# Attention with sorted blocks and a Fourier mixer: keys of two heads in one tile, block means inside the first transform

## The chip, the cores and the metric

One Trainium2 chip, one of its cores. The metric is the device time of one execution in microseconds (us). The engines are named as in the profile: PE is TensorE's matrix multiply and PEld its weight load, DVE is VectorE, ACT is ScalarE, POOL is GpSimd, SP is SyncE, which here only issues DMAs.

## The reference, cut to what matters

```python
# q, k, v: (4, 8, 768, 64); sort_net: (4, 8, 8, 8); 8 blocks of 96 rows
P = sort_net; five rounds of: exp, divide by row sums, divide by column sums
k_sorted = einsum('bhij,bhjcd->bhicd', P, k_blocks)      # the same for v
scores = 0.125 * q_block @ k_sorted_block.T              # inside each block of 96
attn = softmax(scores);  x = attn @ v_sorted_block       # (4, 768, 512) over all heads
u = x + real(fft(fft(x, axis=1), axis=2))
un = (u - mean(u)) / sqrt(var(u) + 1e-6)
out = u + relu(un @ w_ch1) @ w_ch2                       # 512 -> 2048 -> 512
```

## The kernel before

Four batches (b) pass one after the other through the same stages. Every stage is recorded as a list of steps, each with an engine or a choice of engines, a cost, the tiles that it reads and writes, and a priority worked out from its batch and the length of the work behind it. A list scheduler (class `Plan`) then writes the instruction order of all engines. A table of due times per step name and batch, `LEAD`, shifts the priorities. Once written, each engine's order is fixed: an engine that waits for an operand holds everything behind it.

The stages that matter here, with their step names and lines before:

- `means(b)`: sums of v over positions become block means. `psaT` (L638) makes them with 64-wide weights, DVE writes them as a high and a low float16 part into `amt` (L645, L646), and `psA` (L632) turns them into `a16`. The attention is worked out without its mean: `vo` subtracts `a`, and the mean's part of the output is added again later.
- `q_mix` (`psQ`, L707) turns q around, two heads in one tile `qT` of 128 rows (64 rows of each head). `k_mix` (`psK`, L726) sorts k the same way into PSUM, and two evictions (`kz`, L480 on ACT or L484 on DVE) write it to `kzs[hp]`, which has one half of its columns for each head; the other head's 64 rows are zero there. So a product of `qT` with a half of `kzs` over all 128 rows takes the right head alone.
- Scores, one head (all 8 blocks) at a time. Batches 0 and 1: `maxima` (`psS`, L784), then `scores`, in which eight products bring in minus the maximum (L800) and eight the scores (`psT`, L803), exp on ACT (L808), minus one into `eT`. Batches 2 and 3: `turned` (`psS`, L821), exp with the maximum as bias (L826), and a transposing DMA from `es` to `eT` on SP's queue (L845). `values` (`psN`, L868) multiplies by the sorted v in `vs`, which came over DMAs (L690), and DVE normalises into `xr` (L874, L875).
- `fold` (L892, L897) adds and subtracts the two halves of the sequence, `dft_s` (`psWo` L913, `psWe` L925 to L934) is the transform over the sequence, by tables `cso` and `cse` of 96 rows, four blocks to a product group; its results are `W`.
- `mean_path`: `psM` (L746, L751) transforms the means over the model axis by `cdh` and its low part `cdl`, `mh` (ACT) and `tm` (L759, DVE) evict them. `dft_d` (`psF`, L966 to L982) is the transform over the model axis; its first product (L966) adds the means' part by the table `lm`.
- `residual`, `add_res` on POOL (L1032, L1033), statistics, `un`, and its transposes into `unT`, by PE (L1101) or a DMA (L1091).
- `mlp`, for two groups of 384 rows in each batch: 64 products of L1129 and 48 of L1150 for a group. Its priority lies behind all attention steps of later batches, so it fills what they leave free.

Of the kernel before, what the change touches and what calls it, by code (L numbers as in the profile page):

```python
# [9 lines left out]
F32 = mybir.dt.float32  # L10
F16 = mybir.dt.float16
# [5 lines left out]
H = 8  # L17
# [3 lines left out]
BLK = 96  # L21
G = 6
# [22 lines left out]
def _consts():  # L45
# [9 lines left out]
    cd_lo = (cd - cd_hi.astype(np.float64)).astype(np.float16)  # L55
    chunk = lambda m: np.ascontiguousarray(
        m.reshape(2, 128, 2, 3 * LT).transpose(1, 0, 2, 3))
    cd_hi, cd_lo = chunk(cd_hi), chunk(cd_lo)
# [17 lines left out]
    kall = np.concatenate([kpl.reshape(-1), [384]])  # L76
    sall = np.arange(S)
    anga = 2.0 * np.pi * ((sall[:, None] * kall[None]) % S) / S
    csum = np.cos(anga).reshape(NB, BLK, 385).sum(1)
    ssum = -np.sin(anga).reshape(NB, BLK, 385).sum(1)  # L80

    lm = np.zeros((128, 2, 2, 385), np.float16)
    for e, m in enumerate((csum, ssum)):
        hi = m.astype(np.float16)
        lo = (m - hi.astype(np.float64)).astype(np.float16)
        for r, w in enumerate((hi, hi, lo, lo, hi, hi)):
            lm[8 * r:8 * r + 8, 0, e] = w
            lm[64 + 8 * r:72 + 8 * r, 1, e] = w
    negm = np.zeros((128, 1), np.float32)
    negm[32:64] = negm[96:128] = -1.0  # L90
# [17 lines left out]
    for r, kr in enumerate(KP):  # L108
# [12 lines left out]
    return (mask8, selj, mask16, cd_hi, cd_lo, cse, cso, lm, negm, vrow, ones, idx, rsel,  # L121
            nident)
# [260 lines left out]
def kernel(  # L383
# [13 lines left out]
    names = ("mask8", "selj", "mask16", "cdh", "cdl", "cse", "cso", "lm", "negm", "vrow", "ones", "idx",  # L397
             "rsel", "nident")
    (mask8_d, selj_d, mask16_d, cdh_d, cdl_d, cse_d, cso_d, lm_d, negm_d, vrow_d, ones_d,
     idx_d, rsel_d, nident_d) = [  # L400
# [44 lines left out]
    ring("xs", 2, [BLK, 4, 128], F16)  # L445
    ring("x4", 2, [BLK, 2, 2, 128], F16)
# [13 lines left out]
    ring("mh", 1, [128, 2, 2 * LT], F16)  # L460
# [103 lines left out]
    lm = const.tile([128, 2, 2, 385], F16, name="lm_sb")  # L564
    junk = lm[:, 0].rearrange("p e k -> p (e k)")[:, 0:DM]
# [16 lines left out]
    kzs = [const.tile([128, 2, S], F16, name=f"kz{i}") for i in range(4)]  # L582

    def clear_kz(i):
        nc.scalar.activation(kzs[i].rearrange("p h s -> p (h s)"),
                             junk[:, 0:1].broadcast_to([128, 2 * S]), AF.Copy, scale=0.0)
# [10 lines left out]
    cse = const.tile([BLK, 2, 386], F16, name="cse_sb")  # L597
    nse = const.tile([BLK, 2, 192], F16, name="nse")
    cso = const.tile([BLK, 4, 384], F16, name="cso_sb")
    cdh = const.tile([128, 2, 2, 3 * LT], F16, name="cdh_sb")  # L600
    cdl = const.tile([128, 2, 2, 3 * LT], F16, name="cdl_sb")
    negm = const.tile([128, 1], F32, name="negm_sb")
# [13 lines left out]
    amt = const.tile([128, 4, 128], F16, name="amt")  # L616
    a16 = const.tile([128, DM], F16, name="a16")
    amr = const.tile([128, 4, 128], F16, name="amr")
    tm = const.tile([128, 2, 2 * LT], F16, name="tm")
# [6 lines left out]
    def means(b):  # L626
# [12 lines left out]

        def gT(e):  # L640
            ps = bank(pT, [128, 4, NB])
            amv = amt[:, :, 64 * (b % 2):64 * (b % 2) + 64].rearrange(
                "p t (x y i) -> p t x y i", x=4, y=2)
            pTb = ps[:, :, None, :].broadcast_to([128, 4, 4, NB])
            nc.vector.tensor_copy(amv[:, :, :, 0, :], pTb)  # L645
            nc.vector.tensor_tensor(amv[:, :, :, 1, :], pTb, amv[:, :, :, 0, :], op=ALU.subtract)  # L646
# [6 lines left out]
            ("amt", b, {"V": 640}, gT, [pT], [("amt", b % 2)]))  # L653
        plan.chain(
            ("psA", b, {"T": 260}, fA, ["amr"], [pA]),
            ("a16", b, {"A": 585, "V": 685}, lambda e: copy(e, a16, bank(pA, [128, DM])), [pA], ["a16"]))

# [58 lines left out]
    def k_mix(b, hp):  # L716
# [12 lines left out]
        def ev(e, hh):  # L729
            r = slice(64 * hh, 64 * hh + 64)  # L730
            copy(e, kzs[hp][r, hh].rearrange("x (i g c) -> x i g c", g=G, c=16),
                 six(r).rearrange("x g (c i) -> x i g c", c=16), SCALE if b < TURN else -SCALE)
        plan.chain(("psK", b, {"T": 545}, f, [k16[b, hp], (kron[b], hp // 2)], [pK]),
                   *[("kz", b, {"A": 790, "V": 950}, lambda e, hh=hh: ev(e, hh), [pK],
                      [("kz", hp, hh)]) for hh in range(2)])

    def mean_path(b, e_):
        if e_ == 0:
            mh[b] = Buf("mh")
        pM = Buf("bank")  # L740

        def f(e):
            ps = bank(pM, [128, 2 * LT])
            for c in range(2):
                for ci, cc in enumerate((cdh, cdl)):
                    nc.tensor.matmul(ps, amt[:, c, :], cc[:, c, e_, LT:],  # L746
                                     start=(c == 0 and ci == 0), stop=False, skip_group_check=True)
            for c in range(2):
                for ci, cc in enumerate((cdh, cdl)):
                    for y in range(2):  # L750
                        nc.tensor.matmul(ps[:, LT * y:LT * y + LT], amt[:, 2 + c, :],  # L751
                                         cc[:, c, e_, LT * (1 - y):LT * (2 - y)],
                                         start=False, stop=(c == 1 and ci == 1), skip_group_check=True)
        amts = [("amt", y) for y in range(2)]
        plan.chain(
            ("psM", b, {"T": 900}, f, amts + ["cdh", "cdl", "negm"], [pM]),
            ("mh", b, {"A": 372, "V": 400}, lambda e: copy(e, mh[b].t[:, e_, :], bank(pM, [128, 2 * LT])),
             [pM], [(mh[b], e_)]),
            ("tm", b, {"V": 480}, lambda e: nc.vector.scalar_tensor_tensor(  # L759
                tm[:, e_, :], mh[b].t[:, e_, :], negm, bank(pM, [128, 2 * LT]),  # L760
                op0=ALU.mult, op1=ALU.add), [pM, (mh[b], e_)], [("tm", e_)]))
    mh = {}
# [11 lines left out]

    def maxima(n):
        b, h = divmod(n, H)
        hp, hh = h // 2, h % 2
        mxs[n] = Buf("mxs")
        pS = Buf("pair")

        def f(e):
            ps = pair(pS, BLK, 128)
            for i in range(NB):
                nc.tensor.matmul(ps[0:wide(i).stop - BLK * i, i // 4, i % 4], qT[b, hp].t[:, wide(i)], kzs[hp][:, hh, cols(i)])  # L784
        plan.chain(
            ("psS", b, {"T": 370}, f, [qT[b, hp]] + [("kz", hp, hh)], [pS]),
            ("max", b, {"V": 945}, lambda e: nc.vector.tensor_reduce(
                mxs[n].t.rearrange("p (t j) -> p t j", t=2), pair(pS, BLK), axis=AX.X, op=ALU.max),
                [pS], [mxs[n]]))

    def scores(n):
        b, h = divmod(n, H)
        hp, hh = h // 2, h % 2
# [3 lines left out]
        def f(e):  # L797
# [4 lines left out]
            for i in range(NB):  # L802
                nc.tensor.matmul(ps[0:wide(i).stop - BLK * i, i // 4, i % 4], kzs[hp][:, hh, wide(i)], qT[b, hp].t[:, cols(i)],  # L803
                                 start=False, stop=True, skip_group_check=True)
# [5 lines left out]
                [pS], [sms[n]]))  # L810

    def turned(n):
        b, h = divmod(n, H)
        hp, hh = h // 2, h % 2
        eT[n] = Buf("eT")
        et, mn, sm, pS = eT[n], Buf("mns"), Buf("sm"), Buf("pair")
# [581 lines left out]
```

## Time and profile before

| | |
|---|---|
| time, median of 3 runs | 316.94 us (312.82, 316.96, 316.94) |
| span of the profiled execution | 312.2 us (no other time of this execution is given) |
| busy PE / PEld | 287.7 us (92%) / 181.9 us (58%) |
| busy DVE / ACT / POOL | 218.6 (70%) / 206.3 (66%) / 137.8 us (44%) |
| mean granted PE clock | 0.985 |
| chain that ended last | PE 59%, DVE 15%, ACT 8%, DMA 5%, issue 5% |

A busy PE in this table includes the latency of a product's last columns, so it is no measure of streaming; the distance between the starts of products in a full queue is. The chain is followed back from the last instruction to what released it at each step. A group's line gives its number of instructions, busy time, mean ns of one, and the idle time of its engine just before.

### The profile page before, as it was taken

Reading aid. Unit: us, or ns where it says so; the run is one execution under the profiler, and the core shown is the slowest. Engines: PE = TensorE matmul, PEld = TensorE weight load, DVE = VectorE, ACT = ScalarE, POOL = GpSimd, SP = SyncE. Lnnn points to the kernel's source line nnn. Section 1 sums busy time; section 2 is a strip of 40 time slices with the busy share of each in tenths; the row PEclk is TensorE's granted clock in tenths of the full one; section 3 lists DMA queues with packets and bytes.
Section 4 is the critical chain, followed back from the end, with each engine's and each line's share of the span. In section 5 each row is a group of like instructions: output and inputs, shape, how many; then the busy total and the mean of one; then the engine's idle time right before and its main releaser. Section 6 shows DMA issues by size and latency. Waiting matters only on the chain.

```text
span 312.2 us, 7389 instructions
## 1 busy us (share of the span) xinstructions
PE 287.7 (92%) x2715; PEld 181.9 (58%) x2715; DVE 218.6 (70%) x489; ACT 206.3 (66%) x486; POOL 137.8 (44%) x206
## 2 busy tenths in 40 slices
PE   8879599999999798999998999999999999999990
PEld 5657577866765454555654767646556755645540
DVE  6779779998997888787579999997466764010010
ACT  6587587999884567998676759887715754704500
POOL 8634166957125899446444115462021763112020
PEclk9999979999999999999999999999999999999996
DMA  7975886999699776996997444569334337314021
GB/s 214 172 189 92 172 208 96 171 207 219 129 141 213 194 229 111 144 243 171 180 225 132 104 119 96 147 188 212 75 92 135 104 100 215 80 67 136 0 101 35
DMA packets 54396, 45.72 MB, mean 146 GB/s; under 512 B 23393, under 2 KB 46144, under 8 KB 54360
## 3 DMA queue, kind: packets, MB, share of 16 engines
q1 hardware_dynamic: 39560, 28.68, 36.0%
q0 software_dynamic: 14800, 16.57, 30.6%
q8 instruction: 21, 0.34, 0.5%
q14 instruction: 15, 0.12, 0.2%
HBM read 35.33 MB, written 12.58 MB: 153 GB/s over the span
## 4 chain that ended last, share of the span: by engine, by line
PE 59%; DVE 15%; ACT 8%; DMA 5%; issue 5%; POOL 4%; SPq 1%; POOLq 0%; DVEq 0%; ACTq 0%
PE bank L1129 21%; PE bank L1150 21%; DVE kz L484 3%; PE bank L913 3%; DMA v<-in_v_dram 2%; DMA eT<-es 2%; ACT kz L480 2%; PE bank L868 2%; POOL u L1032 1%; POOL u L1033 1%; PE bank L982 1%; PE bank L821 1%; DVE xr L875 1%; ACT un L1075 1%; SPq L690 1%
## 5 line engine op out<-in xcount | busy, mean ns | idle before, releaser
L1129 PE MATMUL bank<-unT,w1sb 128*128 128x384 f16 x512 | 90.8, 326 | 1.3 <-ACT hr L1135 1.3
L1150 PE MATMUL bank<-w2sb,hr 128*128 128x512 f16 x384 | 90.5, 379 | 0.6 <-DVE W L482 0.6
L1135 ACT ACTIVATE hr<-bank 128x384 f16<-128x384 f32 x128 | 60.4, 495 | 28.6 <-PE bank L1129 27.6
L1129 PEld LDWEIGHTS <-w1sb 128*128 128x128 f16 x512 | 48.3, 98 | 31.8 <-issue 2.0
L1173 POOL DMA_INDIRECT out_dram<-outt,idx_sb x23 | 23.1, 1005 | 81.9 <-DVE outt L1158 61.5
L1150 PEld LDWEIGHTS <-hr 128*128 128x128 f16 x384 | 35.9, 98 | 38.3 <-issue 0.8
L1158 DVE SCALAR_TENSOR_TENSOR outt<-ur,bank 128x512 f32<-128x512 f32 x24 | 16.4, 682 | 38.8 <-PE bank L1150 38.8
L826 ACT ACTIVATE sm<-bank,mns 96x96 f32<-96x96 f32 x128 | 32.6, 354 | 4.8 <-DVE mns L831 4.6
L1050 DVE BATCH_NORM_STATS2 st<-u 96x6 f32<-96x512 f32 (+1 forms) x32 | 21.9, 683 | 4.2 <-POOL u L1033 4.0
L875 DVE TENSOR_TENSOR xr<-bank,rz 96x512 f16<-96x512 f32 x32 | 22.0, 686 | 1.1
L1032 POOL TENSOR_TENSOR u<-u,P 96x257 f32<-96x257 f32 (+1 forms) x16 | 11.9, 743 | 22.8 <-DVE P L990 10.9
L524 POOL TENSOR_TENSOR v<-v 128x384 f32<-128x384 f32 x11 | 11.1, 1013 | 18.3 <-ACT v L478 18.2
L484 DVE TENSOR_SCALAR kz<-bank 64x768 f16<-64x768 f32 x16 | 15.2, 952 | 4.9 <-ACT kz L480 3.4
L478 ACT COPY u<-bank 96x512 f32<-96x512 f32 (+1 forms) x21 | 12.1, 586 | 9.0 <-PE bank L1009 6.5
L1075 ACT ACTIVATE un<-u,nm,rstd 96x512 f16<-96x512 f32 (+1 forms) x16 | 13.0, 819 | 6.9 <-DVE nm L1064 6.9
L913 PE MATMUL bank<-cso_sb,xs 96*128 96x384 f16 x64 | 13.4, 332 | 3.9 <-ACT sm L808 2.7
L478 ACT CAST W<-bank 128x384 f16<-128x384 f32 (+1 forms) x29 | 10.6, 402 | 8.6 <-PE bank L913 6.1
L682 DVE SCALAR_TENSOR_TENSOR vo<-a,bank 128x384 f16<-128x384 f16 x32 | 15.7, 542 | 0.0
L480 ACT ACTIVATE kz<-bank 64x768 f16<-64x768 f32 x16 | 12.7, 803 | 4.3 <-DVE kz L484 3.2
L831 DVE TENSOR_REDUCE mns<-bank 96x8 f32<-96x768 f32 x16 | 14.9, 943 | 0.7 <-PE bank L821 0.7
L892 DVE TENSOR_TENSOR xs<-xr 96x512 f16<-96x512 f16 x32 | 14.6, 469 | 0.7 <-PE bank L929 0.2
L808 ACT ACTIVATE sm<-bank 96x768 f32<-96x768 f32 x16 | 12.8, 800 | 3.5 <-PE bank L803 2.8
(149 smaller groups left out, 539.9 us busy)
## 6 DMA issues: line engine op xcount, KB each, us to landing
u_dram<-u SPq DMA_DIRECT2D x32, 192.0 KB
ur<-u_dram SPq DMA_DIRECT2D x24, 256.0 KB
v<-in_v_dram SPq DMA_DIRECT2D x11, 384.0 KB
vs<-vo SPq DMA_DIRECT2D x48, 65.0 KB
k<-in_k_dram POOLq DMA_DIRECT2D x15, 192.0 KB, 4.4
q<-in_q_dram POOLq DMA_DIRECT2D x15, 192.0 KB, 5.0
w1sb<-in_moe_w_ch_dram POOLq DMA_DIRECT2D x4, 512.0 KB, 6.9
w2sb<-in_moe_w_ch_dram POOLq DMA_DIRECT2D x4, 512.0 KB, 6.0
```

The costliest lines, as they stand in the source:

```text
L478: nc.scalar.copy(dst, src)
L480: nc.scalar.activation(dst, src, AF.Copy, scale=scale)
L484: nc.vector.tensor_scalar(dst, src, scale, None, op0=ALU.mult)
L826: nc.scalar.activation(sm.t[:, i], pair(pS, BLK)[:, y, i % 4], AF.Exp, bias=mn.t[:, i:i + 1], scale=-1.0)
L875: nc.vector.tensor_tensor(xr2[b % 2][0:BLK, :, D * h:D * (h + 1)].rearrange("p (t j) d -> p t j d", t=2), ps[:, :, :, 0:D], r[:, :, :, Non ...
L913: nc.tensor.matmul(ps, xs[b, hp, 1].t[:, j, :], cso[:, j, :], start=(j == 0), stop=(j == 3))
L1050: nc.vector.bn_stats(st.t[0:n], us[b, i, m].t[0:n])
L1129: nc.tensor.matmul(ps, w1sb[:, mc, 128 * fc:128 * fc + 128], unT[b, gr].t[:, mc, :], start=(mc == 0), stop=(mc == 3))
L1135: nc.scalar.activation(dst, bank(pH, [128, 384]), AF.Relu)
L1150: nc.tensor.matmul(ps, hr[f4].t[:, fc % 4, 128 * t:128 * (t + 1)], w2sb[:, fc, :], start=(fc == 0), stop=(fc == 15))
L1158: step("outt", b, {"V": 687}, lambda e, t=t, pC=pC, o=o: nc.vector.scalar_tensor_tensor(o.t, ur[t].t, RSC, bank(pC, [128, DM]), op0=ALU.mu ...
L1173: step("store", b, {"G": 1050}, lambda e: nc.gpsimd.indirect_dma_start(out=out.rearrange("b s m -> (b s) m"), out_offset=bass.IndirectOffs ...
```

## The change

The zero halves of `kzs` go: each tile holds 64 rows of one head and 64 of the other, is written by one eviction, and is no longer cleared. A score step no longer takes eight blocks of one head but four blocks (`y`) of both heads of a pair, and each product runs over the 64 rows of one head, the heads taking turns. `values` follows the same grouping, and so does the normalisation.

The mean path goes (`psM`, `mh`, `tm`, the product L966, the tables `lm`, `cdl`, `negm`). Instead the tiles that the first transform reads (`xso`, `xse`, now kept for a whole batch) have 24 more rows: the block means' high part twice and their low part, against 24 more rows of `cso` and `cse` that hold the block sums of the transform's factors. `psB` brings the means to those rows (16 products with 32 weights into PSUM rows 96 to 127), one copy takes them to `xso` (`xom`), one more to `xse` (`xem`). Of the four blocks of a product group the first runs over 120 rows, the others over 96.

The planner's costs for the new steps are given anew; the table `LEAD` is as before.

```diff
-    kzs = [const.tile([128, 2, S], F16, name=f"kz{i}") for i in range(4)]
-    def clear_kz(i): ...
+    kzs = [const.tile([128, S], F16, name=f"kz{i}") for i in range(4)]
...
-        def ev(e, hh):
-            r = slice(64 * hh, 64 * hh + 64)
-            copy(e, kzs[hp][r, hh]..., six(r)..., SCALE if b < TURN else -SCALE)
+        def ev(e):
+            copy(e, kzs[hp]..., six(slice(0, 128))..., SCALE if b < TURN else -SCALE)
...
-            for i in range(NB):
-                nc.tensor.matmul(ps[0:wide(i).stop - BLK * i, i // 4, i % 4],
-                                 qT[b, hp].t[:, wide(i)], kzs[hp][:, hh, cols(i)])
+    def products(ps, left, right, hp, y, start):
+        for j in range(4):
+            for hh in range(2):
+                r, w = slice(64 * hh, 64 * hh + 64), wide(4 * y + j)
+                nc.tensor.matmul(ps[0:w.stop - w.start, hh, j], left[r, w],
+                                 right[r, cols(4 * y + j)],
+                                 start=start, stop=True, skip_group_check=True)
...
+        def fB(e):
+            for t in range(4):
+                nc.tensor.matmul(pB.t[BLK:128, 128 * t:128 * t + 128], amt[:, t], ident)
...
+            ("psB", b, {"T": 260}, fB, ["amt"], [pB]),
+            ("xom", b, {"A": 585, "V": 685}, lambda e: copy(
+                e, xso[b % 2][BLK:KM, :, 0, :], ...), [pB], [("xom", b % 2)]))
+        step("xem", b, {"V": 420}, more, r=[("xom", b % 2)], w=[("xem", b % 2)])
...
-    def mean_path(b, e_): ...
...
+        rows_of = lambda j: KM if j == 0 else BLK
-                    nc.tensor.matmul(ps, xs[b, hp, 1].t[:, j, :], cso[:, j, :],
-                                     start=(j == 0), stop=(j == 3))
+                    n = rows_of(j)
+                    nc.tensor.matmul(ps, x[0:n, j], cso[0:n, j, :], start=(j == 0), stop=(j == 3))
...
-                nc.tensor.matmul(ps[0:n], lm[:, b % 2, e_, k0:k0 + n], tm[:, e_, :], start=True,
-                                 stop=False, skip_group_check=True)
...
-            ("psS", b, {"T": 370}, ...      -            ("psT", b, {"T": 730}, ...
+            ("psS", b, {"T": 190}, ...      +            ("psT", b, {"T": 550}, ...
-            ("psF", b, {"T": 680 if b else 1100}, f,
+            ("psF", b, {"T": 460 if b else 880}, f,
...
-        for h in range(H):
-            n = H * b + h
+        for hp in range(4):
+            for y in range(2):
+                n = b, hp, y
```

More of the change, by code (lines that the diff above doesn't have):

```diff
@@ L727, in f @@
                                      kron[b].t[:, 2 * hp + hh].rearrange("p c i -> p (c i)"))
[L729 to L732 removed]
+        def ev(e):
+            copy(e, kzs[hp].rearrange("x (i g c) -> x i g c", g=G, c=16),
+                 six(slice(0, 128)).rearrange("x g (c i) -> x i g c", c=16), SCALE if b < TURN else -SCALE)
         plan.chain(("psK", b, {"T": 545}, f, [k16[b, hp], (kron[b], hp // 2)], [pK]),
[L734 to L762, printed above, removed]
+                   ("kz", b, {"A": 790, "V": 950}, ev, [pK], [("kz", hp)]))
     mxs, sms, eT = {}, {}, {}
@@ L1332 @@
             mix(0)
-        if b in (0, 1):
-            for y in range(2):
-                mean_path(b, y)
         if b + 1 < B:
```

231 lines of the change are left out of this document (109 added, 122 removed).

## The prediction

> **What bounds the kernel now.** I read the page first: the span, the engines' shares, the slices and the chain that ended last; then busy time by stretches of time; then the groups by line with shapes kept apart; then the timeline of TensorE (PE) where the changed steps stand. The page:
>
> ```profile
> span 312.2 us, 7389 instructions
> PE 287.7 (92%) x2715; PEld 181.9 (58%) x2715; DVE 218.6 (70%) x489; ACT 206.3 (66%) x486; POOL 137.8 (44%) x206
> PE   8879599999999798999998999999999999999990
> PEclk9999979999999999999999999999999999999996
> PE 59%; DVE 15%; ACT 8%; DMA 5%; issue 5%; POOL 4%; SPq 1%; POOLq 0%; DVEq 0%; ACTq 0%
> ```
>
> PE is busy nearly everywhere and is 59% of the chain. The stretches show where that is a bound and where it only looks so:
>
> ```profile
> 30.00:40.00 10.00, 6.57 (x114) 5.69 (x111) 7.35 (x16) 6.24 (x10) 1.73 (x3) 1.00 0.86 179
> 40.00:50.00 10.00, 9.72 (x111) 7.21 (x109) 8.44 (x19) 8.35 (x16) 5.08 (x8) 0.83 0.77 173
> 60.00:70.00 10.00, 8.85 (x101) 6.51 (x99) 9.62 (x26) 9.14 (x21) 7.09 (x11) 1.00 1.06 200
> 100.00:110.00 10.00, 8.40 (x78) 4.83 (x77) 8.40 (x16) 5.23 (x12) 8.49 (x12) 1.00 0.81 183
> 160.00:170.00 10.00, 8.58 (x101) 4.84 (x100) 9.29 (x15) 7.14 (x19) 6.46 (x10) 1.00 0.98 176
> 180.00:200.00 20.00, 20.00 (x179) 13.39 (x178) 19.35 (x48) 16.42 (x53) 6.70 (x9) 1.00 0.50 129
> 262.00:301.00 39.00, 39.00 (x214) 20.77 (x213) 5.11 (x9) 15.68 (x32) 5.30 (x6) 1.00 0.29 93
> ```
>
> The columns are the stretch, its length, busy PE, weight loads, DVE, ACT, POOL (each with a count), the granted clock, the DMA share and GB/s. Up to about 70 us PE waits for DVE, ACT and DMAs. From then on the MLP products fill every hole that the attention leaves, from 180 us PE is full, and from 262 us only MLP is left:
>
> ```profile
> 262.62 10.40 PE bank L1129 x64
> 273.02 10.36 PE bank L1150 x48
> ```
>
> These pieces of the chain, in order of time, give a product's price in a full queue: 10.40/64 = 0.1625 us for 384 columns and 10.36/48 = 0.216 for 512 (the group means of section 5 hold the latency too). So the end is the sum of what PE must stream, plus its waits before 180 us. Work taken from PE shortens the run wherever it lies after 70 us; work taken from DVE or ACT only where PE waits.
>
> **The change, part by part.**
>
> *The mean path on PE goes.* Its rows, and the timeline where they run:
>
> ```profile
> L746 PE MATMUL bank<-cdh_sb,amt 128*128 128x258 f16 x12 | 3.0, 273 | 0.0
> L751 PE MATMUL bank<-cdh_sb,amt 128*128 128x129 f16 x24 | 3.0, 220 | 0.0
> L966 PE MATMUL bank<-tm,lm_sb 128*96 128x258 f16 x24 | 6.5, 273 | 0.3 <-DVE P L990 0.3
> 30.69 0.28 PE L746 MATMUL bank<-cdh_sb,amt 128*128 128x258 f16 x1
> 30.80 0.27 PE L746 MATMUL bank<-cdl_sb,amt 128*128 128x258 f16 x1
> 31.14 0.28 PE L751 MATMUL bank<-cdh_sb,amt 128*128 128x129 f16 x2
> 31.25 0.28 PE L751 MATMUL bank<-cdl_sb,amt 128*128 128x129 f16 x2
> ```
>
> Starts lie 0.11 us apart for 258 columns and 0.055 for 129. With the equal groups on cdl that is 24 x 0.11 + 48 x 0.055 = 5.3 us; on L966 there are 32 products (24 of 96 rows, 8 of 97), 32 x 0.11 = 3.5 us. **-8.8 us.** In exchange the first transform's products get 120 rows instead of 96 for one of its four blocks:
>
> ```profile
> L913 PE MATMUL bank<-cso_sb,xs 96*128 96x384 f16 x64 | 13.4, 332 | 3.9 <-ACT sm L808 2.7 <-DVE xs L892 1.0
> L678 PE MATMUL bank<-v,kron 128*128 128x384 f16 x32 | 6.9, 326 | 0.1
> L632 PE MATMUL bank<-ident,amr 128*128 128x128 f16 x16 | 1.6, 220 | 0.3
> 20.61 0.38 PE L632 MATMUL bank<-ident,amr 128*128 128x128 f16 x4
> ```
>
> A product of 384 columns takes 332 ns with 96 rows and 326 with 128: rows are free. The new step psB is 16 products of the shape of L632, (0.38 - 0.22)/3 = 0.053 us each: **+0.9 us**.
>
> *The scores.* Now, 384 products (L784, L803, L821, 128 each):
>
> ```profile
> 53.94 0.51 PE L800 MATMUL bank<-nident_sb,mxs 96*128 96x96 f16 x8
> 54.28 0.51 PE L803 MATMUL bank<-qT,kz 128*128 128x96 f16 x8
> 112.11 1.14 PE L1129 MATMUL bank<-unT,w1sb 128*128 128x384 f16 x6
> 113.18 0.53 PE L726 MATMUL bank<-kron,k 128*64 128x128 f16 x12
> 113.64 0.42 PE L1012 MATMUL bank<-xr,rsel_sb 99*96 99x512 f16 x1
> ```
>
> Eight take 0.34 us, 0.0425 each, 16.3 us in all. The change makes no fewer of them: each fills 64 of 128 rows, and two neighbours use different halves. Whether two halves of rows run at once, no row shows. Halves of columns do: L726's twelve products of 128 columns and 64 weights take 0.46 us from their start to the next group's, where one after the other they would need 12 x 0.053 = 0.64. I take the pairs at once, 0.047 us a pair (0.0425 and a few ns for the second's start): 192 x 0.047 = 9.0, **-7.3 us**. Bounds: -8.2 (0.0425 a pair) and 0 (not at once).
>
> The same rows show a price. Six products of L1129 from 112.11 end their streaming at 112.11 + 6 x 0.1625 = 113.09, and L726 starts at 113.18: 0.09 late. Within the group, 0.46 is 0.14 more than six pairs at 0.053. So going into half-array products and out again costs some 0.19 us, about 0.095 a turn. In the order in which the instructions of the two programs stand on PE, the shape of the array in use (whole, halves by column, halves by row, psB's quarter) turns 49 times before and 129 times after, since the score steps stand singly among whole-array products: 37 runs of them, 30 of eight. 80 x 0.095 = **+7.6 us**. Bounds: 0, if halves by row turn freely, and 80 x 0.11 = 8.8.
>
> [...]
>
> *DVE and ACT.*
>
> ```profile
> L484 DVE TENSOR_SCALAR kz<-bank 64x768 f16<-64x768 f32 x16 | 15.2, 952 | 4.9 <-ACT kz L480 3.4 <-PE bank L726 0.9 <-ACT a L478 0.5
> L480 ACT ACTIVATE kz<-bank 64x768 f16<-64x768 f32 x16 | 12.7, 803 | 4.3 <-DVE kz L484 3.2 <-DVE a L482 0.5 <-PE bank L726 0.4
> L759 DVE SCALAR_TENSOR_TENSOR tm<-mh,negm_sb,bank 128x258 f16<-128x258 f16 x6 | 2.8, 477 | 0.6 <-ACT mh L478 0.6
> L478 ACT CAST mh<-bank 128x258 f16<-128x258 f32 x6 | 2.2, 384 | 1.5 <-PE bank L751 1.5
> L478 ACT CAST a<-bank 128x512 f16<-128x512 f32 x3 | 1.7, 579 | 0.0
> L646 DVE TENSOR_TENSOR amt<-bank,amt 128x128 f16<-128x128 f32 x4 | 1.2, 291 | 0.1
> 38.78 0.81 PE bank L913 x4
> ```
>
> Thirty-two evictions of kz become sixteen of the same length and twice the partitions: (15.2 + 12.7)/2 = 14 us less over both engines. tm and mh drop 5.0; psB's four copies (priced as `a`, 0.58) and the four copies into xse (some 0.5) add 4.3. Behind 70 us all of this hides under the MLP products and counts nothing. Before 70 us PE's own share of the gain, 3.4 us of L746 and L751 for batches 0 and 1 and part of L966, needs DVE and ACT to move up as well. Half of the kz saving, 7 us over two engines, falls there, 3.5 an engine, so I let the PE terms stand and add nothing. Without that cover some 3 us of the gain would stay behind.
>
> *Moved and added waits; queues.* psB waits for DVE's two amt operations (291 ns each at most), and behind it on PE stands a q transpose, whose eviction leads to the maxima: half a microsecond once a batch, under MLP products in three of four. The first transform now waits for psB's copies too; the 18 us from L632 at 20.61 to the first L913 at 38.78 cover them. On SP the loads of lm, cdl and negm go (0.8 MB by their shapes), those of cse and cso grow by a quarter, and cdh's load falls behind the three copies of `a` into xr; its first reader, the second transform, comes behind that L913. The clearing of kz on POOL and ACT stands ahead of waits for v and for the sort net's chain, so taking it away frees nobody. All nothing.
>
> *The order.* One scheduler places every step from due times per step name, and these are kept. Before 180 us PE's waits may shrink by 3 (DVE and ACT lighter) or grow by 10 (first rival's price and a bit); I take 0, as the MLP tail after the last transposes is alike in both orders (64, 48, 64, 48 products).
>
> Sum: -8.8 + 0.9 - 7.3 + 7.6 = **-7.6 us**, so a span of 304.6. The page has no other time of the profiled execution. The fastest shown run, 312.82, is its span and 0.6; the other two lie 4.1 higher and are the median, 316.94, and no row tells why. I apply the difference to the median: **309.3 us** (-2.4%).
>
> **The rivals.**
>
> *PE meets a transposed eT too early (slower).* Place: batches 2 and 3, the values step L868, behind which all of PE queues.
>
> ```profile
> 29.80 7.38 DMA v<-in_v_dram
> 151.15 6.42 DMA eT<-es
> L868 PE MATMUL bank<-vs,eT 97*128 97x65 f16 x224 | 11.8, 199 | 0.8 <-DMA vs<-vo 0.7
> ```
>
> A flight of 6.42 us stands on the chain, yet L868 waited 0.8 in all: the kept due times put enough MLP ahead. They were set for steps of one head; a step is now half of two. If PE stands through a flight, the clock follows: after the 3.4 idle us of 30 to 40 it was 0.83 for 10 us, 1.7 us lost. One full stand is 8.1, two are 16.2: 325.5 us. From the second on it is slower than before. For it: due times not renewed. Against it: 0 wait after 180 us today and a lighter DVE.
>
> *The row halves do not run at once.* Then the 7.3 goes and the turns stay: 316.6, no change. For it: no row shows row halves. Against it: column halves do.
>
> *The clock gate in the early stage.* The change takes 1.8 us of products out of 30.69 to 32.5, where PE is idlest. If the clock then drops twice more at 1.7, that is 3.4 us: 312.7. Against it: one drop today. [...]
>
> **How the numbers follow.** Forecast 0.51, early eT 0.27, row halves 0.11, clock 0.11. Faster by over 2% (below 310.6; about what a measurement of this kernel can tell from no change): 0.42 of the forecast and 0.02 of the clock case, 0.44. Slower (above 323.3): 0.23 of the eT case. Within: 0.33. The range runs from 303 (turns half as dear and 3 us of waits gone) to 323, which leaves most of the second stand outside. The forecast's own range is 303 to 315.
>
> **What would show it.** Right: score groups of eight take about 0.17 us from first to last pair, with 0.09 lost on each side; PE full from 180 us; L746, L751 and L966 gone and nothing new above 1 us on PE; about 14 us less of kz; the first L1129 three to five us before 69. Wrong: second products of a pair starting 0.042 after the first (row halves); L868 waiting for eT (first rival); clock below 1.00 in more than one stretch after 10 us; turns without the 0.09, which would bring 302.

## The result, and the profile after

The changed kernel takes 321.65 us (median of five; 320.18 to 324.51), the kernel before 314.67 on the same chip: a ratio of 1.026 with a 95% interval of 1.021 to 1.031. It is slower, where the prediction said faster. The page of the profiled execution, the longest of the five at 324.51 us:

```profile
span 322.7 us, 7192 instructions
PE 291.4 (90%) x2627; PEld 176.0 (55%) x2627; DVE 214.3 (66%) x485; ACT 194.0 (60%) x470; POOL 133.5 (41%) x202
PE   8885889797968899979999999999999999999990
PEclk9999579978976599999999999999999999999996
PE 65%; DVE 11%; DMA 10%; POOL 6%; ACT 4%; issue 3%; POOLq 0%; SPq 0%; DVEq 0%; ACTq 0%
```

DVE, ACT and POOL all have less to do, as forecast, and DMA's share of the chain has doubled. The line that stands out is PEclk: before, the clock fell once (a 7); now it falls four times, and a slice goes down to 5. The stretches that answer to those of before (length, busy PE, weight loads, DVE, ACT, POOL, clock, DMA share, GB/s):

```profile
30.00:40.00 10.00, 6.55 (x73) 5.02 (x74) 5.22 (x13) 5.20 (x7) 0.00 (x0) 0.54 0.94 206
60.00:70.00 10.00, 7.94 (x129) 6.12 (x127) 8.83 (x23) 8.57 (x17) 8.85 (x13) 0.92 0.96 182
90.00:100.00 10.00, 7.79 (x91) 6.33 (x92) 5.63 (x16) 6.26 (x11) 0.93 (x2) 0.61 0.77 145
100.00:110.00 10.00, 7.31 (x56) 4.66 (x54) 6.51 (x18) 4.27 (x11) 2.84 (x6) 0.67 0.54 95
180.00:200.00 20.00, 20.00 (x179) 11.50 (x177) 19.47 (x42) 10.95 (x32) 5.09 (x6) 1.00 0.68 159
```

From 180 us on PE is full, as it was. All damage is done before 113 us. Two stands open it; the timeline of PE, then the waits of PE grouped by what ended them (in all, times, longest):

```profile
27.87 0.52 PE L758 MATMUL bank<-kz,qT 64*128 64x96 f16 x16
29.17 0.34 PE L758 MATMUL bank<-qT,kz 64*128 64x96 f16 x8
33.45 1.56 PE L842 MATMUL bank<-vs,eT 97*128 97x65 f16 x24 [3.94 <-DMA vs<-vo]
92.21 1.56 PE L842 MATMUL bank<-vs,eT 97*128 97x65 f16 x24 [2.58 <-DMA vs<-vo]
PE bank L842 <- DMA vs<-vo: 6.5, 2, 3.9
PE bank L627 <- POOL vg L521: 1.8, 1, 1.8
```

The same two places before:

```profile
33.34 0.94 PE L868 MATMUL bank<-vs,eT 97*128 97x65 f16 x24 [0.69 <-DMA vs<-vo]
80.97 0.94 PE L868 MATMUL bank<-vs,eT 97*128 97x65 f16 x24
```

The first values step of batch 0 begins at the same moment in both kernels, 33.4 us: the moves of v into `vs` set it. Before, PE came to it through the mean products (30.69 to 32.5) and waited 0.69. Now the score steps end sooner, the mean products are gone, and PE stands 3.94. The time saved there has become a wait. Batch 1's values step, in contrast, really is 11 us later.

To see what the difference is made of I added up the distances between the starts of all products of a trace. Each distance is split into the product's price at full clock (0.1625 us for 384 columns, 0.216 for 512 and in proportion; 0.0425 for 96; 0.028 for one of 64 weights, 0.022 for one of a pair of row halves), then, where the clock is half, what lies above that, up to the price once more (two products of L1105 start 0.320 us apart there, 0.162 at full clock), then gaps of up to 0.2 us, and waits above 0.2. In us, each row adding up with 1.47 to the start of the last product:

| kernel (profiled execution) | streaming | half clock | small gaps | waits | last product |
|---|---|---|---|---|---|
| before | 264.8 | 1.5 | 12.9 | 23.1 | 303.8 |
| changed | 249.0 | 14.8 | 19.6 | 29.3 | 314.2 |
| difference | -15.8 | +13.3 | +6.7 | +6.2 | +10.4 |

PE has 15.8 us less to stream and ends 10.4 later. Streaming is a count of products times a price, not a measurement of its own; the other three columns are what the trace leaves over: they say where time went, not what caused it. The profiled execution of the changed kernel is its longest, with the lowest clock of the five (0.934; the others 0.944 to 0.954), and the spans of the two traces lie 10.5 us apart where the medians lie 7.0; so its half clock is above the usual. Divided by time with the same rule (to about 1 us), 4 of the 26 us in these three columns arise before 45 us, 20 from 45 to 113 us (half clock +10, waits +9) and 2 behind that. Most is lost in batch 1's stage, not at batch 0's stand.

### The profile page after: what moved, and what is told of

Its sections match the earlier page's. It is cut to its first block, busy times and chain, and to the rows that moved or that the text cites. A ratio compares the mean times of both kernels' runs of the same rounds, so it can differ in the third digit from the quotient of the medians.

```text
span 322.7 us, 7192 instructions
## 1 busy us (share of the span) xinstructions
PE 291.4 (90%) x2627; PEld 176.0 (55%) x2627; DVE 214.3 (66%) x485; ACT 194.0 (60%) x470; POOL 133.5 (41%) x202
## 4 chain that ended last, share of the span: by engine, by line
PE 65%; DVE 11%; DMA 10%; POOL 6%; ACT 4%; issue 3%; POOLq 0%; SPq 0%; DVEq 0%; ACTq 0%
PE bank L1126 22%; PE bank L1105 20%; DMA vs<-vo 5%; PE bank L888 5%; PE bank L842 3%; DMA out_dram<-outt,idx_sb 3%; PE bank L758 2%; DMA u_dram<-u 2%; PE bank L910 2%; PE bank L958 2%; POOL u L1008 2%; DVE mxs L768 2%; PE bank L715 2%; POOL u L1009 1%; PE bank L780 1%
## 5 line engine op out<-in xcount | busy, mean ns | idle before, releaser
L1105 PE MATMUL bank<-unT,w1sb 128*128 128x384 f16 x512 | 90.9, 329 | 1.8 <-DVE vo L690 1.7
L1105 PEld LDWEIGHTS <-w1sb 128*128 128x128 f16 x512 | 48.9, 99 | 34.0 <-issue 3.3
L797 ACT ACTIVATE sm<-bank,mns 96x96 f32<-96x96 f32 x128 | 31.8, 348 | 1.2 <-DVE mns L803 1.0
L473 ACT CAST W<-bank 128x384 f16<-128x384 f32 (+1 forms) x39 | 13.0, 374 | 22.0 <-PE bank L888 9.0
L848 DVE RECIPROCAL rz<-bank 96x8 f32<-96x8 f32 x32 | 6.3, 198 | 22.2 <-PE bank L842 16.0
L842 PE MATMUL bank<-vs,eT 97*128 97x65 f16 (+1 forms) x256 | 14.5, 215 | 6.7 <-DMA vs<-vo 6.5
L842 PEld LDWEIGHTS <-eT 97*128 97x128 f16 (+1 forms) x256 | 13.5, 116 | 10.3 <-DMA vs<-vo 4.1
L827 ACT ACTIVATE eT<-sm 96x768 f16<-96x768 f32 x16 | 13.3, 841 | 6.8 <-PE bank L842 6.5
L888 PE MATMUL bank<-cso_sb,xso 120*128 120x384 f16 (+1 forms) x64 | 17.0, 400 | 0.2 <-issue 0.2
L473 ACT COPY u<-bank 96x512 f32<-96x512 f32 (+1 forms) x19 | 11.1, 593 | 7.4 <-PE bank L985 4.8
```

What stands on the lines that cost most here:

```text
L473: nc.scalar.copy(dst, src)
L797: nc.scalar.activation(sm.t[:, i], pair(pS, BLK)[:, t, i % 4], AF.Exp, bias=mn.t[:, i:i + 1], scale=-1.0)
L888: nc.tensor.matmul(ps, x[0:n, j], cso[0:n, j, :], start=(j == 0), stop=(j == 3))
L1105: nc.tensor.matmul(ps, w1sb[:, mc, 128 * fc:128 * fc + 128], unT[b, gr].t[:, mc, :], start=(mc == 0), stop=(mc == 3))
```

## The experiments

Five readings were tried against each other. **A**: the order. The scheduler's kept due times make a poor order for the new steps, PE stands, and the clock falls. **B**: half-filled products by themselves let the clock fall. **C**: the mean products had kept the clock up. **D**: the changed operations cost more than their streaming, in any order. **E**, which came out of the middle runs: the changed kernel has too little for PE to do early on, in any order. Ratios are to the kernel before on the same chip (312.5 to 315.0 us there), with 95% intervals.

### Full rows in the same order, a held load, filled waits, the keys alone

```diff
e1_full_rows (the order unchanged on all engines)
-    nc.tensor.matmul(ps[..., hh, j], left[r, w], right[r, cols(4 * y + j)], ...)
+    nc.tensor.matmul(ps[..., hh, j], left[:, w], right[:, cols(4 * y + j)], ...)
e2_kq_held, ahead of the load of q for batch 1, pair 1
+    for x in vs[0:2]:
+        nc.gpsimd.tensor_copy(landed, x[0:BLK, 0, 0:1])
e3_filled, in values()
+    for _ in range({(0, 0, 0): 18, (1, 0, 0): 12}.get(n, 0)):
+        nc.tensor.matmul(pN.t[:, 0, :], junk[:, 0:128], junk)
e5_keys_only: before, with kzs, products, maxima, scores, turned, values as changed
```

> The changed kernel with one thing altered: each score product multiplies all 128 rows of the two-head key tile instead of the 64 rows of its head (so both heads get the sum of their scores). Same instructions in the same order on every engine, no row halves, no pairs, no turns of the array for them. Theory A (the order: bulk loads stand ahead of the moves of the values, TensorE stands, its clock falls to half): the waits at L842 (6.5 us) and the stretches of half clock stay; a pair costs 0.085 us instead of 0.042, 192 of them, +8, the turns go, -8: 318 to 326 us. Theory B (half-filled products by themselves let the clock fall): the clock stays full, the 13 us of half-clock streaming come back: 308 to 314 us.

> The changed kernel; on POOL the loads of q and k for batch 1, head pair 1 (at 25.99 and 26.72 us) are held until batch 0's values have been moved into vs. Nothing else moves. Theory A: the 3.9 us of TensorE's wait at L842 near 29.5 us shrink below 1, the stretch of half clock from 30.8 to 44.5 us goes down to 7 us or less, and the run gains 3 to 8 us: 314 to 319. Theory B: the wait shrinks but the clock falls all the same: gain of 0 to 3. If neither the load nor the wait matters because DVE and ACT bound that stage: 320 to 323.

> The changed kernel with products whose result is overwritten put before the first values step of batch 0 (18 of 512 columns, 3.9 us) and of batch 1 (12, 2.6 us), where TensorE stood waiting for vs. They need no vs, so the waits stay as long as they are but TensorE is busy in them. Theory A with the clock as the price: the stretches of half clock from 30.8 and from 92.3 us go (7 to 9 us of streaming come back), the waits stay: 313 to 318. If the waits themselves are the price and the clock is not: 321 to 323. Theory B: the drops come all the same, 321 to 323.

> The kernel before with only the keys' half of the change: two heads in one key tile, scores by 64-row products, steps of half of two heads; the mean path of before stays. The scheduler places the steps anew with its kept due times. By my sum (-7.3 for pairs, +7.6 for turns, mean path unchanged): 315 to 318 if the order were as good as before. Theory A (the loss is in the order that comes out, whichever part causes it): waits above 2 us for vs or eT and more than 10 us of half clock, 318 to 326. Theory C (the mean products that were taken away had kept TensorE's clock up): one stretch of half clock as before, 314 to 318.

*Full rows*: 320.07 us, 1.019 (1.013 to 1.025). A's range, not B's: the waits at L842 stay (5.4 us) and the clock still falls, though less (20.5 us of half clock before the end, against 37.5). Streaming rises by 7.9, small gaps fall from 19.6 to 14.7, half clock from 14.8 to 8.5. Some of the half clock did go with the row halves, so B is not wholly out.

*Held load*: 318.90, 1.015 (1.009 to 1.021). The moves land 2.4 us sooner when the second pair of k/q loads keeps off them, so those loads did cost something, but not the whole wait:

```profile
31.08 1.56 PE L846 MATMUL bank<-vs,eT 97*128 97x65 f16 x24 [1.69 <-DMA vs<-vo]
```

The wait did not go below 1 and the half clock there went from 13.7 to 10.2 us, not 7: A's sign, its size at the edge. B's words fit as well (the wait shrinks, the clock falls all the same, a gain of 0 to 3), for the gain is 2.7 us, on another chip. This run does not part the two.

*Filled waits*: 320.72 (318.03 to 322.44), 1.023 (1.016 to 1.030), a miss for A, and 0.3 us short of the range for waits that cost by themselves. In the profiled execution batch 0 came as A had it: 18 products fill the stand, the values step begins where it did, the clock stays full to 91 us, and PE is 4.1 us ahead by the product that stood at 45.03 us:

```profile
29.48 4.06 PE L841 MATMUL bank<-junk 128*128 128x512 f16 x18
```

But that was the fastest of its four runs, with a mean clock of 0.979; the others had 0.959 to 0.964 and 320 to 322 us, so the clock was down for longer in them; where, no trace shows. Batch 1's half clock, 10.2 us, stayed in the profiled execution too.

*Keys alone*: 321.41, 1.021 (1.011 to 1.030), 17.1 us of half clock although the mean products are there. A's other sign, a wait above 2 us for `vs` or eT, is not there in these words: 1.1 and 0.6 us, and one of 4.0 at a values step that the trace puts down to a load of v. The half clock speaks against C as the whole cause and, with the time, for A.

### What an order is worth

```diff
e6_before_no_due / e7_after_no_due
-    LEAD = dict(P=(37.1, 31.1, 0, 0), ..., weights=(-5.3, 0, 0, 0))
+    LEAD = {}
e8_after_costs: in the changed kernel
-    ("psS", b, {"T": 190}, ...)   ("psT", b, {"T": 550}, ...)
+    ("psS", b, {"T": 370}, ...)   ("psT", b, {"T": 730}, ...)
e9_before_costs: the reverse in the kernel before
```

> The kernel before, with every due time of the scheduler's table set to zero; same work, another order. Theory A (what the change lost, it lost because due times fitted to the old steps were kept): this loses too, 318 to 332 us. Theory D (the changed operations themselves cost more than their streaming shows, whatever the order): no statement on this one; it is the base for the next.

> The changed kernel, also with every due time set to zero, so that neither kernel has an order fitted to it. Theory A: the change now shows what its work is worth, 3 to 10 us faster than the kernel before without due times. Theory D: it stays 5 to 10 us slower than that one.

> The changed kernel with the due times kept, but the scheduler is told 370 and 730 ns for the two score steps on TensorE, as for the old steps, instead of 190 and 550: what a step of eight products with its two turns really takes by the traces (0.36 and 0.71 us). If the order is poor because these costs are too low: waits at the values step under 2 us, 309 to 316. If it is poor because the due times do not fit: 316 to 324.

> The kernel before with the wrong costs of 190 and 550 ns told to the scheduler for its score steps: not one instruction is added or taken away, only the order is made anew. Theory A: 317 to 324 us, with more waits and more half clock than before. Theory D: 312 to 316.

The last is the plainest: the same operations as before (six moved from ACT to DVE), two numbers told wrongly to the scheduler, and 325.28 us, 1.039 (1.030 to 1.047), a little more than A's range. Its page:

```profile
span 321.8 us, 7385 instructions
PEclk9999999959699999999999999999999999999997
```

Without any due times the kernel before takes 324.51, 1.038 (1.031 to 1.045), and the changed one 322.34, 1.031 (1.024 to 1.038). So the kernel before loses 12 us with its fitted order, as A had it. By the sums above, its waits are then some 8 us longer and its half clock 3 (with the wrong costs 7 and 4): in this kernel a poor order costs waits first and clock second. Without due times the changed one is 0.7% ahead (2.2 us), short of A's 3 to 10. D, which had it 5 to 10 us behind, falls. Telling the scheduler the true length of the new score steps brings the changed kernel from 1.026 to 1.015 (1.008 to 1.022; 317.45 us): the given costs had left the turns out. By its expectation (309 to 316 or 316 to 324) the larger part is then in the due times, not in those costs.

### Orders fitted to the changed kernel

```diff
e10_refit, e11_refit_b, e12_refit_c: e8 with another table each
-    LEAD = dict(P=(37.1, 31.1, 0, 0), Q=(0, 1.3, 0, -8.4), ...)
+    LEAD = dict(P=(0, 183.2, 41.2, 3.1), Q=(-27.6, -56.7, 23.1, -39.0), ...)
e13_costs_filled: e8, and in values()
+    for _ in range({(0, 0, 0): 18}.get(n, 0)):
+        nc.tensor.matmul(pN.t[:, 0, :], junk[:, 0:128], junk)
```

> The changed kernel with the scheduler's due times fitted to it anew (its own table, chosen so that TensorE has work in each stretch of 3.4 us from 20 us on) and the score steps told at 370 and 730 ns. The same operations, another order. Theory A (the change's own work is worth some 9 us, and the old due times gave that and more back): below the kernel before, 304 to 312 us, with fewer than 15 us of half clock. Theory E (the changed kernel has too few products before 110 us to keep the clock up in any order): 313 to 320, with half clock between 30 and 45 us as in every kernel so far that has the row halves.

> As the run above, with a second table of due times, found from another start. Theory A: 304 to 314 us; the two tables differ by less than the 12 us that lie between the fitted and the unfitted order of the kernel before. Theory E: 313 to 320.

> As the two above, with a third table. Theory A: 305 to 315 us. Theory E: 313 to 320.

> The kernel with the old due times and the score steps told at 370 and 730 ns (317.45 us in its run), and 18 products of 512 columns, whose result is overwritten, before the first values step of batch 0, where TensorE stands waiting for vs in the stretch before the clock falls at 31.9 us. If half clock in the early stage costs time by itself: the stretch from 31.9 to 45.6 us goes (5.3 us of streaming), and the run gains 2 to 5 us: 312 to 315.5. If DVE, ACT and the moves set the pace there whatever the clock: 316.5 to 319.

312.49, 313.22 and 314.04 us: 0.999 (0.995 to 1.003), 0.999 (0.993 to 1.004) and 1.000 (0.995 to 1.006). That is 2.6 to 2.7% better than the kept table, and all three are level with the kernel before, none below. The times lie at the upper ends of A's ranges (the first half a us above): what the lower ends stood for, nine us less for PE, does not show. E's range overlaps, and its sign is there in all three:

```profile
span 309.6 us, 7184 instructions
PEclk9997569999998999999999999999999999999996
24.17:27.59 3.42, 2.40 (x60) 1.73 (x58) 3.42 (x5) 1.82 (x3) 2.95 (x7) 1.00 0.57 114
27.59:31.00 3.41, 2.78 (x40) 2.12 (x37) 2.44 (x3) 2.49 (x4) 1.33 (x2) 0.50 1.12 161
31.00:44.65 13.65, 12.72 (x127) 9.52 (x128) 8.89 (x22) 8.94 (x14) 2.69 (x4) 0.50 0.75 170
```

This is the first fitted order. In the stretch from 24.17 us, batch 0's score steps, DVE is busy throughout (3.42 of 3.42) and sets the pace; PE, with score products that take half the time, streams for 0.37 of it by the prices above, and the clock is half for the next 17 us.

The filled run missed: 320.79, 1.023 (1.017 to 1.029), where the run without filling had 1.015; slower if anything, as the intervals overlap. In its profiled execution the clock had already fallen at 27.7, so the 18 products took 6 us where PE had 2.64 to wait:

```profile
30.47 6.02 PE L841 MATMUL bank<-junk 128*128 128x512 f16 x18
33.09 1.56 PE L842 MATMUL bank<-vs,eT 97*128 97x65 f16 x24 [2.64 <-DMA vs<-vo]
```

The first row is of this run, the second of the run without filling. It came out above both alternatives, and as a test of the price of half clock it says nothing.

### Which half of the change

```diff
e14_refit_filled (count 1, 1) and e15_refit_filled_more (2, 2, and 6 in values): e10, batch 0
+    fill(pS, count)      # ahead of the products of psS, and of psT
e16_refit_full_rows: e10 with the edit of e1; e18_refit_b_full_rows: e11 with it
e4_means_only: before, with with_means, psB, xom, xem, fold, dft_s as changed, no mean_path
e17_means_refit: the same with its own LEAD, psS and psT at 370 and 730
```

> The changed kernel with the first refitted table (312.49 us), and in batch 0 one product of 512 columns, whose result is overwritten, before the products of each of the 16 score steps: 0.22 us each, about what a step lost when its products began to run in pairs (0.17). They run while TensorE waits for DVE's maxima. Theory E, sharpened (score steps of half the length leave TensorE busy in less than 0.45 of a stretch of 3.4 us near 25 us, and the clock then stays half for 10 to 17 us): half clock before 50 us falls from 17 to 7 us or less, and the run gains 2 to 5 us: 307 to 311. If that half clock lies under DVE and ACT anyway: 312 to 316.

> As the run above with two such products in each of the 16 score steps and six before the first values step, 8.2 us of them in all before 45 us. Theory E, sharpened: the clock stays full to 80 us; gain of 2 to 5 us less what does not fit under waits: 308 to 313. If half clock there costs nothing: 313 to 319.

> The first refitted order with score products over all 128 rows (both heads get the sum of their scores), no row halves, the same instructions in the same order. TensorE streams 8 us more and saves 5 of turns. Theory E, sharpened: the clock falls later or less than with the halves, and the time is 309 to 314, no more than with them: pairs gain nothing in this order. If the pairs are worth their streaming: 314 to 318.

> The changed kernel in the second refitted order (313.22 us) with score products over all 128 rows (both heads get the sum of their scores): the third order in which row halves and full rows stand in the same order. In the two others full rows were 0.6 to 0.7% below. If row halves gain nothing in any order: 309 to 313 us. If that was chance: 315 to 318 (8 us more streaming, 5 less of turns).

> The kernel before with only the means' half of the change: the 24 rows in the first transform instead of the mean path, keys and scores by head over 128 rows as before (the folded tiles are kept once, not twice, for want of memory). The order is made anew with the kept due times. By my sum (8.8 us of products out, 0.9 in): 305 to 308 us if the order were as good as before. Theory A: the order that comes out costs as much as it did the others, 316 to 326.

> The same with due times fitted to it. No row halves, so no turns for them and score steps of full length. If what the change lost after refitting lies in the row halves alone (they stream 8 us less, but turns and half clock take that back): the 8 us of the means show and the run comes to 303 to 309, below both kernels. If saved products before 110 us only lengthen the waits for moves, DVE and ACT, or the fit by hand is worse than the old one: 310 to 316.

*Filled score steps*: 313.66, 1.002 (0.998 to 1.006), and 313.41, 1.001 (0.997 to 1.005). The second did keep the clock up through the early stage, and gained nothing. The whole stretch, the first values step and a group of the first transform, each in the filled run and then in the first fitted order, and between them the last maxima on DVE in the filled run:

```profile
20.00:45.00 25.00, 24.69 (x344) 15.12 (x344) 19.66 (x38) 16.57 (x26) 9.93 (x14) 1.00 0.66 140
20.00:45.00 25.00, 21.52 (x282) 15.74 (x280) 19.04 (x38) 16.06 (x23) 9.96 (x14) 0.66 0.71 150
35.36 0.94 PE L857 MATMUL bank<-vs,eT 97*128 97x65 f16 x24
31.93 1.56 PE L851 MATMUL bank<-vs,eT 97*128 97x65 f16 x24 [1.35 <-DMA vs<-vo]
30.22 2.70 DVE L781 TENSOR_REDUCE mxs<-bank 96x8 f16<-96x768 f32 x3 [1.52 <-PE bank L771]
44.19 0.82 PE L903 MATMUL bank<-cso_sb,xso 120*128 120x384 f16 x4
44.91 0.82 PE L897 MATMUL bank<-cso_sb,xso 120*128 120x384 f16 x4
```

Clock 1.00 against 0.66 over 25 us, and the group of the first transform that stands at 44.91 us in the fitted order comes at 44.19, 0.7 us ahead. The times are those of the second alternative, and the gain of 2 to 5 us of the sharpened E did not come. But this does not show that half clock is free. The filling holds PE for 24.69 of the 25 us, DVE waits for PE's scores, and the first values step comes 3.4 us later than without filling. From there to that group the fitted order takes 13.0 us at half clock and the filled run 8.8 at full. In *filled waits* the same stage, begun at the same moment, gained 4.1. So half clock did cost some 4 us here, and the filling took most of that again.

*Full rows in two fitted orders*: 310.96, 0.993 (0.989 to 0.998), and 312.25, 0.990 (0.986 to 0.994).

```profile
span 308.9 us, 7184 instructions
PEclk9999999999999999999999999999999999999997
22.15:25.56 3.41, 3.02 (x54) 2.14 (x53) 3.41 (x9) 2.52 (x4) 2.78 (x3) 1.00 0.37 100
25.56:28.98 3.42, 3.01 (x58) 2.54 (x56) 3.42 (x6) 1.56 (x2) 2.95 (x6) 1.00 0.52 114
```

This is the first of them, among the same score steps: PE busy for 3.0 of 3.41 and the clock never down before the end. In three orders now, full rows are 0.7, 0.6 and 0.9% *below* the row halves; each pair's intervals overlap, but the sign is the same three times. The table shows where the time went in the profiled executions:

| order | | streaming | half clock | small gaps | waits | last product |
|---|---|---|---|---|---|---|
| kept due times | halves | 249.0 | 14.8 | 19.6 | 29.3 | 314.2 |
| | full rows | 256.9 | 8.5 | 14.7 | 29.4 | 310.9 |
| first fitted | halves | 249.0 | 7.8 | 18.2 | 24.7 | 301.1 |
| | full rows | 256.9 | 0.0 | 13.6 | 28.5 | 300.5 |
| second fitted | halves | 249.0 | 7.0 | 18.0 | 27.0 | 302.4 |
| | full rows | 256.9 | 4.2 | 13.6 | 26.7 | 302.8 |

The halves save 7.9 us of streaming, pay 4.4 to 4.9 for turns, and 2.8 to 7.8 in half clock.

*The means alone*: 328.10, 1.037 (1.029 to 1.045) in the order of the kept due times, even above A's range; 312.91, 0.996 (0.993 to 1.000) in one fitted to it. PE has 7.9 us less to stream (256.9 against 264.8), and 0.4% of the time shows. So the first alternative, 303 to 309, fails: the row halves are not the only place where the gain went. Both of these kernels keep the folded tiles once and not twice, which can cost waits of its own; that was not tried apart, nor is it known how good the fit is. In the trace of the fitted one, waits are 3.1 us above those of before, half clock 2.3, small gaps 1.2.

No kernel with the reference's whole computation was below the one before by more than its interval.

## Why the prediction was wrong

**The step that failed** is the one on the order, which bounded PE's waits before 180 us at 3 us less and 10 more and took 0. In the traces waits grew by 6.2, inside the bound, but of the clock the bound held no more than the 1.7 us of one stand: half clock added 13.3. Together 19.5, twice the bound, against a forecast gain of 7.6. The argument for 0, that the MLP tail is alike in both orders, looked at the end, where indeed nothing changed, and not at the stage whose order was remade. Nor did it hold that work taken from PE after 70 us shortens the run wherever it lies: by the sums above, PE streamed some 15 us less from 70 to 113 us than before, and lost as much there in half clock (10) and waits (5). The runs put the fit of an order at 12 us for the kernel before (325.28 and 324.51 against 312.53 with its own order), and at 8 to 9 for the changed one (1.026 against 0.999 to 1.000).

How an order loses it can be read for batch 1, though this was not tried by itself. On POOL, the last two sums of v before; then after: the sum before the last, the first and last of the eight additions that now stand ahead of the last one, and that one itself; then the moves on SP's queue:

```profile
50.31 0.99 POOL L524 TENSOR_TENSOR v<-v 128x384 f32<-128x384 f32 x1 [2.52 <-ACT v L478]
53.10 1.00 POOL L524 TENSOR_TENSOR hr<-hr 128x384 f32<-128x384 f32 x1
54.21 0.99 POOL L519 TENSOR_TENSOR v<-v 128x384 f32<-128x384 f32 x1 [4.68 <-ACT v L473]
57.15 0.74 POOL L1008 TENSOR_TENSOR u<-u,P 97x257 f32<-97x257 f32 x1
63.44 0.72 POOL L1009 TENSOR_TENSOR u<-u,P 96x255 f32<-96x255 f32 x1
64.13 0.99 POOL L519 TENSOR_TENSOR hr<-hr 128x384 f32<-128x384 f32 x1
80.72 11.38 SPq L698 DMA_DIRECT2D vs<-vo  x12
```

The means need that sum, `a16` the means, `vo` needs `a16`, and the moves need `vo`: 11 us on POOL reach the values step as 11 us. About 4 of them were there one sum earlier, behind a cast on ACT; the other 7 are the additions and the loads among them.

**The mean path** was right: -8.8 and +0.9 were -7.9 by count, and the 24 more rows cost nothing: a product of the first transform took 399 ns with 120 rows and 400 with 96, with half clock in both groups:

```profile
L888 PE MATMUL bank<-cso_sb,xso 96*128 96x384 f16 x48 | 13.5, 400 | 0.0
L888 PE MATMUL bank<-cso_sb,xso 120*128 120x384 f16 x16 | 6.4, 399 | 0.2 <-issue 0.2
```

**Pairs**, -7.3, were -7.9: sixteen row-half products take the 0.52 us (row at 27.87 above) that eight full ones took before. The rival that they would not run at once is out. **Turns**, +7.6, were 4.4 to 4.9 in the three pairs of orders. No row of before shows that row halves cost a turn as column halves do: it was the author's estimate, and these 4.4 to 4.9 us, 0.06 a turn, are what the runs showed in its place. (The prediction's 0.09 and 0.14 make 0.23 for two turns, not its 0.19; the rows here make 0.20.) One turn in a full queue is as dear as said:

```profile
57.23 0.50 PE L780 MATMUL bank<-nident_sb,mxs 96*128 96x96 f16 x8
57.67 0.35 PE L758 MATMUL bank<-qT,kz 64*128 64x96 f16 x8
57.85 0.34 PE L758 MATMUL bank<-kz,qT 64*128 64x96 f16 x8
58.12 0.52 PE L780 MATMUL bank<-nident_sb,mxs 96*128 96x96 f16 x8
```

Eight whole products and the turn in take 0.44 us instead of 0.34, eight in pairs and the turn out 0.27 instead of 0.17. But by the sums only those 0.06 us of each of the 80 are left over; the rest presumably lies under waits. So the score part was worth about -3 by itself, and the prediction had it at nothing; in the three pairs half clock stood 2.8 to 7.8 higher with the halves, and the runs with them came out no faster.

**The evictions of kz** were right: 13.8 us after, 27.9 before.

```profile
L475 ACT ACTIVATE kz<-bank 128x768 f16<-128x768 f32 x10 | 8.1, 812 | 7.9 <-PE bank L734 7.7 <-DVE amt L634 0.3
L479 DVE TENSOR_SCALAR kz<-bank 128x768 f16<-128x768 f32 x6 | 5.7, 951 | 2.0 <-PE bank L734 1.3 <-ACT rstd L1037 0.6
```

But "I let the PE terms stand", because DVE and ACT move up with PE, did not follow: the first MLP product, promised three to five us earlier than 69, came at 71.4.

**The rivals.** Early eT had the time nearly right (325.5) for a wrong reason: PE waited 6.5 us for `vs` in batches 0 and 1, and 0.2 for eT. The clock rival had the early stage, a cause that can only be a part (1.8 us of products taken out where PE is idlest; the clock fell in *keys alone* too, which keeps them) and the sign of its test (clock below 1.00 in more than one stretch), and was priced by the one drop of before, twice 1.7. There were four falls, together eleven stretches of 3.41 us.

What stays open: how much of the loss the half clock caused by itself (some 4 us in batch 0's stage, by two filled runs; batch 1's was not kept away in any) and how much it only went along with the waits; and whether an order exists in which the change pays. Three fitted tables and one for the means alone give ratios of 0.996 to 1.000, and the table of before was fitted to its own kernel by means unknown here.

## What to carry to other kernels

When a kernel's order was fitted to its steps, a change of steps starts with the loss of that fit: price it by remaking the order of the *old* kernel (a wrong cost is enough; here 12 us, 4%), before counting what the new steps save. Work taken off the busiest engine in a stage that a DMA paced became a wait here: the stand before the first values step grew from 0.69 to 3.94 us, and the clock from 30 to 40 us was 0.54, where it had been 1.00. A planner's cost for a step should be its distance to the next step's start, turns included: that alone gave back 1.1% here.

## What the runs showed of the hardware

**The clock fell without an idle stretch.** In the traces of before and of the changed kernel every stretch at half clock that ended before the last product lasted 3.413 us or a whole multiple of it: 3.413 before; 13.653, 6.827, 10.240 and 6.827 in the changed kernel. Over the twenty traces of this study, take stretches of 3.413 us laid end to end from a trace's own falls, from 12 us to the last product, and the share of each in which PE streamed (each product at its price above, twice that at half clock). Of the stretches at full clock, the clock fell after 19 of 19 with a share below 0.25, after 34 of 133 from 0.25 to 0.50, and after none of 1,464 above; in the traces of before and of the changed kernel alone, after 2 of 2, 3 of 9 and none of 148. All 53 returns to full followed a stretch at half clock with a share of 0.67 or more; stretches at half clock with less, 16 of them, were each followed by another, and so were 29 with more (in the two traces 5 returns, and 1 and 6). These are counts of this study and no more than that. Four stretches of the changed kernel:

```profile
23.97:27.39 3.42, 2.74 (x68) 2.05 (x67) 3.42 (x6) 2.06 (x3) 3.36 (x7) 1.00 0.72 129
27.39:30.80 3.41, 1.71 (x44) 1.28 (x40) 3.02 (x4) 2.74 (x4) 0.04 (x1) 1.00 1.15 171
30.80:34.22 3.42, 0.77 (x15) 0.80 (x16) 0.04 (x1) 0.05 (x1) 0.00 (x0) 0.50 1.17 247
34.22:44.46 10.24, 10.24 (x113) 7.58 (x111) 6.61 (x17) 6.82 (x11) 2.19 (x4) 0.50 0.43 105
```

PE was busy for half of the stretch just before the fall, and later for all of 10.24 us before the clock came back. Falls stand behind shares of up to 0.48, and the clock stayed at half behind stretches in which PE was busy throughout. From execution to execution the clock differed too: over its 91 executions beside the experiments the kernel before ran with mean clocks of 0.970 to 0.996, and each 0.01 less went with about 2 us more.

**Row halves started together**: in the changed kernel the two products of a pair start 0 to 21 ns apart, 168 of the 192 pairs within 6, and at full clock most pairs of a group follow each other in 41 to 43 ns, 21 a product.
